# Block products given out between the last layer norm's power and its use, and side sums one product earlier

## The chip, the cores and the metric

The kernel runs on one core of one Trainium2 chip, in one launch. The metric is the device time of an execution in microseconds (us), the median of several runs. An execution taken by the profiler also gives a span, from its first to its last instruction, and a trace of every engine: PE is TensorE's matmuls, PEld its weight loads, DVE VectorE, ACT ScalarE, POOL GpSimd, SP the engine that issues the DMAs.

## What is computed

A transformer block with adaptive layer norm, in float32, on 2048 tokens of width 512:

```python
mod = (_silu(c) @ w_mod).reshape(c.shape[0], 6, 1, -1)      # sa, ca, ga, sb, cb, gb
h = _layernorm(x) * (1 + ca) + sa
x = x + ga * _A_ref(h, A_wqkv, A_wo)                        # linear attention, 32 heads of 16
h = _layernorm(x) * (1 + cb) + sb
x = x + gb * _B_ref(h, B_w_gate, B_w_up, B_w_down)          # ((h W) * (h V)) W2, inner width 1376
```

The second layer norm and the gated feed-forward part behind it are what this case is about.

## The kernel before

**Split products.** A float32 operand is split into a high part, rounded to float32r, the type in which TensorE multiplies it, and a low part, the rest (`split`, L182): ACT makes the high part, DVE or GpSimd the low one. A product of two split operands is three matmuls: high by high, low by high, high by low.

**Tiles.** The 2048 tokens are four chunks of 512 (`ch` 0 to 3), each of four tiles of 128 tokens. The inner width of 1376 is eleven column groups of up to 128.

**The feed-forward blocks.** For most column groups gate and up projections are not computed as eight quarter products, but as seven, in the manner of Strassen and Winograd, over a pair of chunks (0, 1) or (2, 3): sums and differences of quarters of the left operand (`Left`, L743: s1 to s4, the "side sums") and of the weights (`Right`, L792). `block` (L856) is one column group for one pair of chunks. It gives out seven products, P1 to P7, with a `yield` behind each; a product is one call of `times` (L833), six matmuls of 128x512 at L838. They accumulate in four banks a, b, c, d of PSUM, which P1 to P7 write in the order a, d, b, a, c, d, c. Between them stand

- `copy(b, a)` after P1, `copy(p5, d)` after P2, `copy(c, b)` and a copy into `u2` after P3: ACT, L843;
- after P5 `p5 = c + p5` (DVE, L893), after P6 `u2 = d + u2` (DVE, L897);
- after P6 and P7 the multiplications of gate and up, `mul(a, u2)` and `mul(c, p5)` (DVE, L866), whose results are split (`kh` on ACT L183, `kl` on DVE L184) only in the next block, after its first bank copy (`flush`).

So P1 of a block can overwrite bank a only when `mul(a, u2)` of the block before has read it, P5 can accumulate in c only when `copy(c, b)` is done, and P7 can only when `p5 = c + p5` has read c.

At named points behind the products (`p1`, `p5`, `p6`, `p2`, `p7`, `p3`, `p4` in the order P1 to P7) other work is hung in: at `p6` the scaling of the next down weights (DVE, L985), at `p7` the loads for coming blocks and the split of the next block's weights (ACT L817 and L820, GpSimd L824), at `p3` the split of the down weights (ACT L183, GpSimd L184), at `p4` the weight sums (GpSimd, L806). The blocks are called b0, b1, b2, ... here; the kernel counts them in `m`.

**The order is written out by hand.** Each engine works through its own queue in the order in which the program gives the instructions out; semaphores hold an instruction until its operands are there, and all behind it on that engine wait with it. `fill(n)` (L1015) gives out the next n products of the feed-forward blocks, with what hangs at their points, in the middle of other code. It is used while the last chunk's layer norm is under way (L1153 to L1165):

```python
    y_b(15)
    norm2[3].rstd_of()
    norm2[3].nmr_of()
    fill(2)
    norm2[3].xhat(0)
    fill(2)
    norm2[3].xhat(1)
    fill(1)
    norm2[3].xhat(2, 3)
    fill(2)
    ln2_turn(3, 0, 1)
    fill(1)
    ln2_turn(3, 2, 3)
```

`y_b` takes the last attention tile out of PSUM and its statistics. `rstd_of` (L228) adds epsilon on DVE (`ve`, L233) and raises to the power -1/2 on GpSimd (`rstd`, L234). `nmr_of` (L236) makes minus mean times that, on DVE (`nmr`, L237). `xhat` (L240) normalizes a tile of tokens on ACT (L243). `ln2_turn` (L727) transposes two of the four column quarters on TensorE (L250, into two PSUM banks), applies scale and shift on ACT (`f`, L262) and, for this chunk, stores them to DRAM (`kept`, L264, a DMA in SP's queue).

Behind this, the left operands of the second pair of chunks are loaded back from `kept` (eight loads `f`, L110, in SP's queue; a load of a stored piece waits until the store has landed), and their side sums, splits and stores for later are put into a list, `trickle` (L1166). Portions of that list, one entry each, are given out by `some` (L963) at several points of each of the blocks b2 to b6: the first entry is s1 of the first half, a DVE addition (L756) of two loaded pieces, the first and the third of the four that the code above stores. In b2 the points `p1` and `p5` are left out.

From b2 on, blocks are followed by down products (L914 to L916).

Of the kernel before, what the change touches and what calls it, by code (L numbers as in the profile page):

```python
# [22 lines left out]
def tile_adaln_block(  # L23
# [162 lines left out]
    def split_raw(raw, shape=(P, D), low=None):  # L186
        h = B("w", shape, F32R)
        l = B("w", shape, F32R)
        split(raw, h[:raw.shape[0]], l[:raw.shape[0]], low)
        return h, l  # L190
# [425 lines left out]
    def y_b(i):  # L616
        ch, j = divmod(i, NJ)
        ps = yps.pop(i)
        nc.scalar.activation(xts[ch][j], ps, AF.Copy)
        norm2[ch].stats(j, of=ps)  # L620
# [160 lines left out]
    def fetch(stash, side, *names):  # L781
        for n in names:
            side[n] = []
            for k in range(KH):
                side[n].append(tuple(B("h", dt=F32R) for _ in range(2)))
                for part, x in enumerate(side[n][k]):
                    nc.sync.dma_start(f32(x), stash[n, k, part])
# [64 lines left out]
    def flush():  # L852
        while todo:
            todo.pop(0)()

    def block(A, R, out, at):  # L856


        n, R = R.n, R.of
        a, b, c, d = (x[:n] for x in banks)  # L860

        def T2(tag):
            return B(tag)[:n]

        def mul(ps, x):
            nc.vector.tensor_tensor(x, ps, x, op=ALU.mult)  # L866
            todo.append(lambda: out.append(split_h(x, n)))

        def also(point):
            for do in at.get(point, ()):  # L870
                do()

        times(a, A["a11"], R["b11"], True)
        copy(b, a)
        flush()
        also("p1")
        yield
        times(d, A["s1"], R["t1"], True)
        p5 = T2("u")
        copy(p5, d)  # L880
        also("p5")
        yield
        times(b, A["s2"], R["t2"], False)
        copy(c, b)
        u2 = T2("u")
        copy(u2, b)
        also("p6")
        yield
        times(a, A["a12"], R["b21"], False)
        also("p2")  # L890
        yield
        times(c, A["s3"], R["t3"], False)
        nc.vector.tensor_tensor(p5, c, p5, op=ALU.add)  # L893
        also("p7")
        yield
        times(d, A["s4"], R["b22"], False)
        nc.vector.tensor_tensor(u2, d, u2, op=ALU.add)  # L897
        mul(a, u2)
        also("p3")
        yield  # L900
        times(c, A["a22"], R["t4"], False)
        mul(c, p5)
        also("p4")
        yield

    def down_group(ch, side, js, outs, ds, last, by_tile=False, end=False):

        hs = [out[side] for out in outs]

        def mm(ps, i, j, c, d):  # L910
            (hh, hl), (dh, dl) = hs[i], ds[i]
            a, b = j * P, (j + 1) * P
            n = hh.shape[0]
            nc.tensor.matmul(ps, hh[:, a:b], dh[:n, c:d], start=i == 0, stop=False)  # L914
            nc.tensor.matmul(ps, hh[:, a:b], dl[:n, c:d], start=False, stop=False)  # L915
            nc.tensor.matmul(ps, hl[:, a:b], dh[:n, c:d], start=False, stop=i == len(hs) - 1)  # L916

        dn = {j: acc_bank() for j in js}
        tail = js[-1:] if end else []
        order = [(i, j) for i in range(len(hs)) for j in js if j not in tail]  # L920
        if by_tile:
            order.sort(key=lambda ij: ij[1])
        for i, j in order:
            mm(dn[j], i, j, 0, D)

        def take():
            evac(ch, dn, [j for j in js if j not in tail], last)
            for j in tail:
                other = acc_bank()
                for ps, c, d in ((dn[j], 0, D // 2), (other, D // 2, D)):  # L930
                    for i in range(len(hs)):
                        mm(ps[:, c:d], i, j, c, d)
                    evac(ch, {j: ps}, [j], last, ((c, d),))
        return take
# [6 lines left out]
    def right_load(n):  # L941
        if n < len(steps):
            rights[n] = Right(steps[n][1])

    def right_sums(n, on=None):
        if n < len(steps):
            rights[n].sums(on)

    def right_split(n, on=None):
        if n < len(steps):  # L950
            rights[n].high()
            rights[n].lows(on)
# [3 lines left out]
    def draw_load(n):  # L956
        if n < len(steps):
            f0, k = fts[steps[n][1]]
            draws[n] = load(w_down[f0:f0 + k, :], "raw")
# [3 lines left out]
    def some(count):  # L963
        for _ in range(min(count, len(trickle))):
            trickle.pop(0)()
# [6 lines left out]
    def ffn():  # L972

        first_side, second_side = side, {}
        m = 0
        for g, (cs, fs) in enumerate(groups):
            last = g + 1 == len(groups) or groups[g + 1][0] != cs
            outs, ds = [], []
            A = first_side if cs == (0, 1) else second_side
            for f in fs:  # L980
                out = []
                draw = draws.pop(m)

                def scale(d=draw):
                    nc.vector.tensor_tensor(d, d, gb[:d.shape[0]], op=ALU.mult)  # L985

                at = {"p6": [scale],
                      "p7": [lambda: draw_load(m + 1), lambda: right_load(m + 2), lambda: right_split(m + 1)],
                      "p3": [lambda: ds.append(split_raw(draw, low=nc.gpsimd))],
                      "p4": [lambda: right_sums(m + 2)]}  # L990
                for point in ("p1", "p5", "p2", "p3", "p4")[2 if m == 2 else 0:]:
                    at.setdefault(point, []).append(lambda: some(some_at.get(m, 0)))
                if m + 1 < len(steps) and steps[m + 1][0] != cs:
                    at["p1"].append(lambda: fetch(stash, second_side, "a11", "s1"))
                    at["p7"].insert(0, lambda: fetch(stash, second_side, "s2", "a12", "s3"))
                elif m and steps[m - 1][0] != cs:
                    at["p1"].append(lambda: fetch(stash, second_side, "s4", "a22"))
                outs.append(out)
                yield from block(A, rights[m], out, at)
                m += 1  # L1000
                if free[0] and parts:
                    takes = [down_group(*p) for p in parts.pop(0)]
                    yield
                    for take in takes:
                        take()
            cut_at = {2: ([[0, 1, 2, 3], []], [[], [0, 1, 2, 3]]),
                      3: ([[0, 1, 2], []], [[3], [0, 1]], [[], [2, 3]])}[len((groups + groups[-1:])[g + 1][1])]
            parts.extend([(ch, i, js, outs, ds, last) for i, (ch, js) in enumerate(zip(cs, jss)) if js] for jss in cut_at)
        flush()
        while parts:  # L1010
            group = parts.pop(0)
            for p in group:
                down_group(*p, by_tile=not parts, end=not parts and p is group[-1])()

    def fill(n):  # L1015
        for _ in range(n):
            next(work, None)
# [121 lines left out]
    draw_load(0)  # L1139
    stash, some_at = {}, {m: 1 for m in range(2, 7)}  # L1140
    work = ffn()
    y_step(14, seed=None)
    fill(1)
# [8 lines left out]
    fill(2)  # L1152
    y_b(15)  # L1153
    norm2[3].rstd_of()
    norm2[3].nmr_of()
    fill(2)
    norm2[3].xhat(0)
    fill(2)
    norm2[3].xhat(1)
# [38 lines left out]
```

## Time and profile before

| what | value |
|---|---|
| median of 3 runs | 570.62 us (570.37 to 571.47) |
| the profiled execution | 570.02 us |
| its span | 568.3 us |
| mean granted TensorE clock | 0.999 |
| TensorE matmuls | 560.3 us busy, 99% of the span, 2575 instructions |
| VectorE | 373.1 us, 66% |
| ScalarE | 279.8 us, 49% |
| GpSimd | 186.2 us, 33% |

Rows of a timeline give the start and the length in us from the span's start, then engine, line, operation, result and operands by the program's names, shapes, the number of instructions merged into the row, and in brackets the idle time of that engine ahead of it with the instruction that ended it. A matmul's end is modelled and matmuls are pipelined, so consecutive rows of TensorE overlap by a fraction of a microsecond; starts are the safer numbers. Rows of the waits give the line that waited, the line it waited for, and total us, number of times and longest. Rows of DMAs give what is moved, the number, KB each, and the us from issue to landing.

The edited place lies at about 285 to 308 us of the span: b0's last product, b1, and b2.

### The profile page before, as it was taken

What the parts mean: (1) busy time and instruction counts of PE and PEld (TensorE: products, weight loads), DVE (VectorE), ACT (ScalarE), POOL (GpSimd) and SP (SyncE); (2) the same over time, 40 slices, a digit from 0 to 9 for tenths busy, and PEclk for the clock granted to TensorE, in tenths of its full rate; (3) what the DMA queues carried; (4) which work ended last, traced back from release to release, by engine and by line L of the source; (5) the groups of instructions that cost most, each with busy time, mean ns of one, the idle gap of its engine ahead of it and who ended that gap; (6) DMA issues with size and microseconds to landing.
All of it is one profiled execution on the core that took longest, in us unless ns stands there. A gap on an engine that the chain in (4) does not pass through costs nothing.

```text
span 568.3 us, 7356 instructions
## 1 busy us (share of the span) xinstructions
PE 560.3 (99%) x2575; PEld 458.8 (81%) x2575; DVE 373.1 (66%) x614; ACT 279.8 (49%) x500; POOL 186.2 (33%) x191
## 2 busy tenths in 40 slices
PE   8999999999999999999989999999999999999997
PEld 6778888888888878878878888787888888888886
DVE  7876868868768876759767777745554434344445
ACT  3785857546456546445865545534333333334110
POOL 2000000000011300000579666665667446556200
PEclk9999999999999999999999999999999999999999
DMA  8900223302301000804208553599336012200004
GB/s 289 374 3 2 74 75 110 114 0 62 93 0 47 29 1 37 260 0 149 57 2 277 180 190 104 202 348 330 115 111 178 26 57 55 57 19 2 0 1 148
DMA packets 50309, 59.34 MB, mean 104 GB/s; under 512 B 6432, under 2 KB 27168, under 8 KB 50272
## 3 DMA queue, kind: packets, MB, share of 16 engines
q1 hardware_dynamic: 50272, 58.87, 32.1%
q8 instruction: 20, 0.33, 0.2%
q14 instruction: 17, 0.14, 0.1%
HBM read 43.12 MB, written 15.73 MB: 104 GB/s over the span
## 4 chain that ended last, share of the span: by engine, by line
PE 89%; DMA 3%; issue 2%; POOL 1%; DVE 1%; ACT 1%; SPq 1%; POOLq 0%; ACTq 0%
PE bank L838 28%; PE acc L914 6%; PE acc L915 6%; PE acc L916 6%; PE acc L614 6%; PE bank L198 5%; PE bank L196 5%; PE bank L197 5%; PE acc L329 3%; PE acc L327 3%; PE acc L328 3%; PE bank L693 2%; PE bank L691 2%; PE bank L692 2%; PE bank L250 2%
## 5 line engine op out<-in xcount | busy, mean ns | idle before, releaser
L838 PE MATMUL bank<-h,w 128*128 128x512 f32 (+1 forms) x798 | 185.5, 390 | 1.8 <-ACT bank L843 1.2
L838 PEld LDWEIGHTS bank<-h,w 128*128 128x128 f32 (+1 forms) x798 | 148.2, 186 | 35.3 <-ACT bank L843 1.7
L843 ACT ACTIVATE bank<-bank 128x512 f32<-128x512 f32 (+1 forms) x38 | 22.1, 583 | 144.8 <-PE bank L838 144.8
L678 DVE TENSOR_TENSOR x<-acc,x 128x512 f32<-128x512 f32 (+1 forms) x73 | 49.1, 684 | 49.0 <-PE acc L916 48.2
L824 POOL TENSOR_TENSOR w<-raw,w 128x256 fp32r<-128x256 f32 (+3 forms) x38 | 42.4, 1117 | 106.4 <-ACT w L817 86.4
L184 POOL TENSOR_TENSOR w<-raw,w 128x512 fp32r<-128x512 f32 (+1 forms) x25 | 34.9, 1399 | 116.0 <-DVE mv L226 87.6
L914 PE MATMUL acc<-w,kh 128*128 128x512 f32 (+2 forms) x154 | 59.6, 387 | 0.0
L915 PE MATMUL acc<-w,kh 128*128 128x512 f32 (+2 forms) x154 | 59.6, 387 | 0.0
L916 PE MATMUL acc<-w,kl 128*128 128x512 f32 (+2 forms) x154 | 59.5, 386 | 0.0
L234 POOL TENSOR_TENSOR rstd<-ve,half 128x4 f32<-128x4 f32 (+1 forms) x9 | 9.4, 1044 | 126.0 <-DVE ve L233 124.5
L184 DVE TENSOR_TENSOR kl<-u,kh 128x512 fp32r<-128x512 f32 (+1 forms) x38 | 26.8, 746 | 33.1 <-ACT kh L183 31.2
L824 POOL TENSOR_TENSOR w<-t,w 128x512 fp32r<-128x512 f32 (+1 forms) x38 | 48.4, 1293 | 0.0
L196 PE MATMUL bank<-w,h 128*128 128x512 f32 x112 | 45.0, 402 | 0.0
L198 PE MATMUL bank<-w,h 128*128 128x512 f32 x112 | 43.9, 392 | 0.0
L197 PE MATMUL bank<-w,h 128*128 128x512 f32 x112 | 43.6, 389 | 0.0
L614 PE MATMUL acc<-w,xh 128*128 128x512 f32 x120 | 38.1, 399 | 0.0
L914 PEld LDWEIGHTS acc<-w,kh 128*128 128x128 f32 (+1 forms) x154 | 28.9, 188 | 6.0
L916 PEld LDWEIGHTS acc<-w,kl 128*128 128x128 f32 (+1 forms) x154 | 28.9, 188 | 5.9
L915 PEld LDWEIGHTS acc<-w,kh 128*128 128x128 f32 (+1 forms) x154 | 28.9, 188 | 5.9
L893 DVE TENSOR_TENSOR u<-bank,u 128x512 f32<-128x512 f32 (+1 forms) x19 | 13.1, 690 | 30.0 <-PE bank L838 30.0
L243 ACT ACTIVATE n<-x,nmr,rstd 128x512 f32<-128x512 f32 x32 | 24.1, 804 | 17.2 <-DVE nmr L237 15.9
L262 ACT ACTIVATE f<-bank,col,col 128x512 f32<-128x512 f32 x28 | 20.7, 775 | 14.5 <-PE bank L250 12.4
(177 smaller groups left out, 1105.1 us busy)
## 6 DMA issues: line engine op xcount, KB each, us to landing
raw<-in_w_mod_dram SPq DMA_DIRECT2D x24, 256.0 KB, 3.7
raw<-in_B_w_down_dram SPq DMA_DIRECT2D x20, 256.0 KB, 2.9
raw<-in_B_w_gate_dram SPq DMA_DIRECT2D x36, 128.0 KB, 3.7
raw<-in_B_w_up_dram SPq DMA_DIRECT2D x36, 128.0 KB, 3.6
x<-in_A_x_dram SPq DMA_DIRECT2D x16, 256.0 KB, 5.4
kept<-f SPq DMA_DIRECT2D x16, 256.0 KB, 2.0
f<-kept SPq DMA_DIRECT2D x16, 256.0 KB, 4.8
side_s<-h SPq DMA_DIRECT2D x16, 256.0 KB, 2.6
```

Source lines behind the costliest of these rows:

```text
L184: (low or nc.vector).tensor_tensor(l, src, f32(h), op=ALU.subtract)
L196: nc.tensor.matmul(ps, ah, bh, start=i == 0, stop=False)
L197: nc.tensor.matmul(ps, ah, bl, start=False, stop=False)
L198: nc.tensor.matmul(ps, al, bh, start=False, stop=i == n - 1)
L243: nc.scalar.activation(self.n[j], self.tiles[j], AF.Identity, scale=self.rstd[:, j:j + 1], bias=self.nmr[:, j:j + 1])
L614: nc.tensor.matmul(yps[i], x, y, start=False, stop=k == KD - 1 and x is al, skip_group_check=True)
L678: nc.vector.tensor_tensor(xt[:, a:b], dn[j][:, a:b], xt[:, a:b], op=ALU.add)
L824: sub = lambda out, x, y: (on or nc.gpsimd).tensor_tensor(out, x, f32(y), op=ALU.subtract)
L838: mm = lambda x, y, **kw: nc.tensor.matmul(ps, x[:, k], y, skip_group_check=True, **kw)
L914: nc.tensor.matmul(ps, hh[:, a:b], dh[:n, c:d], start=i == 0, stop=False)
L915: nc.tensor.matmul(ps, hh[:, a:b], dl[:n, c:d], start=False, stop=False)
L916: nc.tensor.matmul(ps, hl[:, a:b], dh[:n, c:d], start=False, stop=i == len(hs) - 1)
```

## The change

```diff
@@ -988,7 +988,7 @@
                       "p4": [lambda: right_sums(m + 2)]}
-                for point in ("p1", "p5", "p2", "p3", "p4")[2 if m == 2 else 0:]:
+                for point in ("p1", "p5", "p6", "p3", "p4")[2 if m == 2 else 0:]:
                     at.setdefault(point, []).append(lambda: some(some_at.get(m, 0)))
@@ -1152,8 +1152,9 @@
     fill(2)
     y_b(15)
     norm2[3].rstd_of()
+    fill(3)
     norm2[3].nmr_of()
-    fill(2)
+    fill(1)
     norm2[3].xhat(0)
     fill(2)
     norm2[3].xhat(1)
```

Two things are moved.

The portions of `trickle` that stood behind P4 (`p2`) stand behind P3 (`p6`), there behind the scaling of the down weights.

Three products are given out between `rstd_of` and `nmr_of`, and one, no longer two, between `nmr_of` and the first `xhat`. In all, sixteen products are given out by `fill` up to the end of this code, where it was fourteen, so that everything from `nmr_of` on comes later in the order of products:

| given out | before | after |
|---|---|---|
| between `rstd_of` and `nmr_of` | none | P7 of b0, P1 and P2 of b1 |
| between `nmr_of` and `xhat(0)` | P7 of b0, P1 of b1 | P3 of b1 |
| between `xhat(0)` and `xhat(1)` | P2, P3 of b1 | P4, P5 of b1 |
| between `xhat(1)` and `xhat(2, 3)` | P4 of b1 | P6 of b1 |
| between `xhat(2, 3)` and the first two transposes | P5, P6 of b1 | P7 of b1, P1 of b2 |
| between these and the last two transposes | P7 of b1 | P2 of b2 |

No instruction is added or taken away on any engine.

## Prediction

> **What bounds the kernel now.** I read the page's engine line first, then TensorE's waits, then the timelines of single engines around the edit. A "product" below is one `times` call (six matmuls, L838); P1 to P7 are the seven of a block, b0, b1, b2 the first three blocks.
>
> ```profile
> PE 560.3 (99%) x2575; PEld 458.8 (81%) x2575; DVE 373.1 (66%) x614; ACT 279.8 (49%) x500; POOL 186.2 (33%) x191
> ```
>
> ```profile
> PE bank L838 <- ACT bank L843: 1.2, 1, 1.2
> PE bank L257 <- ACT n L243: 0.5, 1, 0.5
> PE bank L838 <- DVE u L866: 0.3, 1, 0.3
> ```
>
> TensorE (PE) is busy 99% of the span, and of its few waits (total us, times, longest) the two for bank copies and multiplications at L838 lie at the edit. So the time is the matmuls plus the few places where TensorE stands still: what an edit saves or adds there goes into the time one to one, and what it does to other engines counts only through TensorE.
>
> ```profile
> 280.68 4.24 PE L838 MATMUL bank<-h,w 128*128 128x512 f32 x18
> 285.23 5.72 PE L838 MATMUL bank<-h,w 128*128 128x512 f32 x24 [0.31 <-DVE u L866]
> 292.19 3.02 PE L838 MATMUL bank<-h,w 128*128 128x512 f32 x12 [1.24 <-ACT bank L843]
> 295.04 1.03 PE L250 MATMUL acc<-ident,n 128*128 128x128 f32 x8
> 295.83 1.63 PE L838 MATMUL bank<-h,w 128*128 128x512 f32 x6
> 297.30 1.03 PE L250 MATMUL acc<-ident,n 128*128 128x128 f32 x8
> 298.09 9.83 PE L838 MATMUL bank<-h,w 128*128 128x512 f32 x42
> 307.76 0.39 PE L914 MATMUL acc<-w,kh 128*128 128x512 f32 x1
> ```
>
> TensorE's timeline (start, length, form, count; idle before it and who ended that). Rows overlap by the pipeline's tail, so I work with starts. The 42 matmuls of b2 take 307.76 - 298.09 = 9.67 us, 0.230 each, 1.38 a product. At this pace the 24 from 285.23 (P1 to P4 of b1) make room for P5 at 290.75; it starts at 292.19. That is 1.44 us of standstill. Likewise b0's last 18 matmuls end at 284.82 and b1's P1 starts at 285.23: 0.41 us.
>
> Who makes P5 late? DVE, then ACT, in order of time:
>
> ```profile
> 284.39 0.69 DVE L866 TENSOR_TENSOR u<-bank,u 128x512 f32<-128x512 f32 x1
> ...
> 285.94 0.34 DVE L233 TENSOR_SCALAR ve<-mv 128x4 f32<-128x4 f32 x1
> 288.50 0.69 DVE L237 SCALAR_TENSOR_TENSOR nmr<-mv,rstd 128x4 f32<-128x4 f32 x1 [2.23 <-POOL rstd L234]
> 289.12 0.68 DVE L866 TENSOR_TENSOR u<-bank,u 128x512 f32<-128x512 f32 x1
> ```
>
> ```profile
> 286.95 0.58 ACT L843 ACTIVATE bank<-bank 128x512 f32<-128x512 f32 x1 [3.43 <-PE bank L838]
> 287.44 0.62 ACT L183 ACTIVATE kh<-u 128x512 fp32r<-128x512 f32 x1
> 289.83 0.63 ACT L183 ACTIVATE kh<-u 128x512 fp32r<-128x512 f32 x1 [1.76 <-DVE u L866]
> 290.37 0.80 ACT L243 ACTIVATE n<-x,nmr,rstd 128x512 f32<-128x512 f32 x1
> 291.07 0.57 ACT L843 ACTIVATE u<-bank 128x512 f32<-128x512 f32 x1
> 291.55 0.58 ACT L843 ACTIVATE bank<-bank 128x512 f32<-128x512 f32 x1
> ```
>
> `nmr_of` (L237) stood 2.23 us in DVE's queue for GpSimd's power. Behind it stood the last product of b0 (L866 at 289.12), behind that ACT's second `kh` (289.83), behind that the first `xhat` and the bank copy that P5 needs (291.55 to 292.13, P5 at 292.19).
>
> **The change part by part.** The program's order, engine by engine, has the same instructions before and after; only places differ. The other edit (side sums at P3, not P4) moves nothing: between the two points stand only TensorE's six matmuls of P4, so DVE, ACT and the DMA queue get their instructions in the same order as before. Its cost is 0, whatever hides it.
>
> *What goes.* `nmr` now stands behind L866 and both `kl` of b0. The power ends at about 288.5 (where `nmr` starts), and by then DVE has work. ACT's queue becomes 286.95 copy, two `kh` to 288.5, then the copy for P5, 0.34 after the product ahead of it ends (b1's P1 ends 286.61, its copy starts 286.95): 290.75 - 1.38 + 0.34 = 289.71, ended 290.29. P5 can start at 290.75: **-1.44 us**. The cover for the power is L866 and the two `kl`, to about 289.4 (the first `kh` ends at 288.06, two `kl` of some 0.7 behind it); it is gone if the power ends later than that, or if ACT's `xhat` gets ahead of the copy, which its order excludes.
>
> *What comes between blocks.* Before, the second four columns of transposes (297.30) lay between b1's P7 and b2's P1 and covered DVE's multiplication L866. Now P1 follows P7 directly, as between b0 and b1, where that cost 0.41. So P5 to P7 run from 290.75 to 294.89, P1 of b2 starts at 295.30: **+0.41 us**. Both transpose groups cost 0.88 each as before (297.30 to 298.09, and 0.09 ahead), one after P1 (296.68 to 297.56), one after P2 (298.94 to 299.82). The first needs all four `xhat`s:
>
> ```profile
> 292.54 2.21 ACT L243 ACTIVATE n<-x,nmr,rstd 128x512 f32<-128x512 f32 x3
> 294.66 0.41 ACT L817 ACTIVATE w<-raw 128x256 fp32r<-128x256 f32 x1
> ...
> 296.53 0.62 ACT L183 ACTIVATE w<-raw 128x512 fp32r<-128x512 f32 x1
> 297.05 2.77 ACT L262 ACTIVATE f<-acc,col,col 128x512 f32<-128x512 f32 x4
> 299.82 0.58 ACT L843 ACTIVATE bank<-bank 128x512 f32<-128x512 f32 x1
> 300.32 1.14 ACT L183 ACTIVATE kh<-u 128x512 fp32r<-128x512 f32 x2
> 301.36 0.59 ACT L843 ACTIVATE u<-bank 128x512 f32<-128x512 f32 x1
> ```
>
> An `xhat` takes 0.71 (three from 292.54 to 294.66), the weight copies of L817 and L820 that now stand behind the first one 1.87 (to 296.53), the `w` split 0.52. From 290.7, when the three bank copies are done, the last `xhat` ends at 290.7 + 4 x 0.71 + 1.87 + 0.52, near 296.0: 0.7 us ahead of its use, and P3 of b2 starts at 299.82. Before it was 298.09 + 2.76 = 300.85. So far TensorE leads by 1.03 us.
>
> *What is late next.* Behind the transposes hang ACT's L262, the stores of the four `f` to DRAM, the loads of the side sums' inputs from there, and the first side sum (L756) on DVE.
>
> ```profile
> 299.17 0.32 SPq L264 DMA_DIRECT2D kept<-f  x1
> ```
>
> ```profile
> 301.29 0.32 SPq L110 DMA_DIRECT2D f<-kept  x1
> ```
>
> ```profile
> f<-kept SPq DMA_DIRECT2D x1, 256.0 KB, 3.4
> ```
>
> ```profile
> 304.80 0.77 DVE L756 TENSOR_TENSOR s<-f,f 128x512 f32<-128x512 f32 x1 [0.38 <-DMA f<-kept]
> 305.49 0.68 DVE L893 TENSOR_TENSOR u<-bank,u 128x512 f32<-128x512 f32 x1
> ...
> 307.99 1.23 DVE L756 TENSOR_TENSOR s<-f,f 128x512 f32<-128x512 f32 x1
> 309.14 0.68 DVE L866 TENSOR_TENSOR u<-bank,u 128x512 f32<-128x512 f32 x1
> ```
>
> The third `f` is the one that counts: evicted from 298.43 (third of four, 0.69 each), stored at 299.17, its load issued 2.12 us later at 301.29 (the load waits for the store to land), landed 3.4 us later at 304.69, and L756, which DVE was already waiting for (0.38 us idle), starts at 304.80. Right behind it in DVE's queue stands L893, which reads bank c for `p5`; P7 of b2 overwrites bank c, so it waits for L893. L893 ended at 306.17; with 0.15 us to TensorE (284.39 + 0.69 to 285.23) that is 306.32, and P7's turn came at 298.09 + 6 x 1.38 = 306.37. **The chain had 0.05 us to spare.**
>
> Afterwards ACT copies b2's P1 at 296.68 + 0.34 = 297.02, does two `kh` (to 298.56, by the steps 299.82, 300.32, 301.36), two L262 (to 299.94), and then, because P2 is given out between the transposes, the copy for `p5` (0.5 us), and only then the third L262: 300.44, which is 2.01 us later than 298.43. Everything behind it moves with it: the store from 299.17 to 301.18, the sum from 304.80 to 306.81, L893 to 307.50 to 308.18, P7 to 308.33. TensorE could give it out at 299.82 + 4 x 1.38 = 305.34 and stands still for 3.0 us. Against 306.37 before, P7 is **1.96 us later**. The sum is the same: -1.44 + 0.41 + 2.99 = +1.96.
>
> Nothing behind takes it back: the down projection and b3 have their operands earlier than TensorE needs them, and TensorE is the bound to the end.
>
> The bounds. If b2's P1 doesn't lose the 0.41 us, ACT's chain starts as much earlier: +1.55. The sum's length depends on GpSimd: 0.69 us from its start to the next DVE instruction in the one row, 1.15 in the other (307.99 to 309.14, GpSimd busy). With the longer one it is +2.42. Both together give +1.55 to +2.42; I take 1.96, from the row of this very instruction. If two more such delays hit the chain it is +2.9.
>
> The Trainium skill (SBUF — State Buffer, "Who interferes with whom") says that a VectorE instruction with two SBUF inputs and a GpSimd instruction that reads SBUF exclude each other for the whole of the earlier one. The 1.23 us of the row at 307.99 agree with it; by the rule the sum would be held for one GpSimd instruction at most, and the time would be near my upper bound.
>
> **The sum against the runs.** The profiled execution took 570.02 us (span 568.3), and with 1.96 comes to 572.0. The timed runs have a median of 570.62, 0.60 above the profiled one, the lowest 0.35 above; I add 0.5 and predict 572.5.
>
> **The rivals.**
>
> *The gain alone.* The store and load of the third `f` come back sooner than in this trace, so that L893 isn't held. For it: two of the four stores now go ahead by more, so the third queues behind less. Against: behind the third nothing changes, and of the 5.5 us from store to landing 3.0 would have to vanish. Then -1.03: 569.6 on the scale of the timed runs. The chain decides at 3.0 us; below that each us counts.
>
> *Half of it.* The wait is there but shorter by 1 to 1.5 us (the load's 3.4 us contain the queue of seven others): +0.5 to +1.0, 571.3.
>
> *A cold array.* TensorE stands still for 3.0 us, twice as long as ahead of P5 now; should its clock drop after that, as it does not here during 1.4:
>
> ```profile
> 290.60:292.20 1.60, 0.36 (x3) 0.02 (x1) 1.60 (x2) 1.60 (x4) 1.60 (x2) 1.00 0.02 5
> ```
>
> (busy time by engine, then the granted clock, 1.00), and halve for as long as the gap lasted, 3.0 us of work would lose 1.5: 574.0. The Trainium skill (TensorE: Matmul & The Clock Gate, "What's actually happening") has such a rule, with an idle window of about 3.4 us; a gap of 3.0 would just stay under it, and nothing in this trace shows what a longer one does.
>
> *The change doesn't do what it says.* `nmr` might still hold something: but by the time the power is ready it still has 0.9 us of other DVE work ahead of it, so the 1.44 us are the safest term. Were they not won, all would come 1.44 later: 573.9.
>
> **How the numbers follow.** The forecast, 571.6 to 573.4 by its own bounds and the runs' scatter: 0.77. Half of it: 0.10. The gain alone: 0.07. A cold array: 0.04. The change not doing what it says: 0.02. The range 571.0 to 573.6 leaves out the gain, the cold array and part of the half. About 0.2%, 1.1 us, is what a measurement of this kernel can tell from no change, so 571.76 is the border: slower 0.76 (most of the forecast and the cold array), within 0.2% 0.16 (the half and the forecast's lower end), faster 0.08.
>
> **What would show it.** Right: no wait of `nmr` for the power and P5 of b1 at 290.7; 0.4 us ahead of b2's P1; DVE idle for the load of `f` for over 2 us ahead of L756 near 306.8; TensorE idle near 3 us ahead of b2's P7, released by L893. Wrong: L893 of b2 near 304.5 with no DMA wait ahead, or a clock under 1.00 after the gap, or a new wait at P5 of b2 (the copy of L843, which I have ending at 302.4, 0.2 us ahead of its use).

## The result, and the profile after

| | before | after |
|---|---|---|
| median | 570.50 us (6 runs, 569.61 to 571.47) | 574.02 us (6 runs, 571.61 to 574.80) |
| ratio, 95% interval | | 1.0056 [1.0036, 1.0076] |
| the profiled execution, its span | 570.02 us, 568.3 us | 573.47 us, 571.8 us |
| mean granted clock, by run | 0.999 in the profiled one | 1.000 (571.61 us), 0.997 (573.47, 574.02, 574.03, 574.33), 0.994 (574.80) |

The change costs 3.5 us. The forecast was 572.5 with a range up to 573.6: the direction was right, and the time lies outside the range.

The engine line of the changed kernel and TensorE's waits (line that waited, line waited for, total us, times, longest):

```profile
PE 561.0 (98%) x2575; PEld 459.2 (80%) x2575; DVE 371.7 (65%) x614; ACT 279.6 (49%) x500; POOL 185.1 (32%) x191
```

```profile
PE bank L838 <- DVE u L893: 3.3, 1, 3.3
...
PE bank L838 <- DVE u L866: 0.6, 2, 0.3
```

The 1.2 us for the bank copy (L843) are gone, and a single wait of 3.3 us for L893 has come. TensorE's timeline of the changed kernel shows both places, and a third thing (start, length, form, count, idle before):

```profile
280.50 4.24 PE L838 MATMUL bank<-h,w 128*128 128x512 f32 x18
285.05 9.81 PE L838 MATMUL bank<-h,w 128*128 128x512 f32 x42 [0.31 <-DVE u L866]
295.17 1.61 PE L838 MATMUL bank<-h,w 128*128 128x512 f32 x6 [0.31 <-DVE u L866]
...
299.67 5.73 PE L838 MATMUL bank<-h,w 128*128 128x512 f32 x24
308.70 2.13 PE L838 MATMUL bank<-h,w 128*128 128x512 f32 x6 [3.30 <-DVE u L893]
310.63 0.63 PE L914 MATMUL acc<-w,kh 128*128 128x512 f32 x1
311.06 0.63 PE L915 MATMUL acc<-w,kh 128*128 128x512 f32 x1
...
313.15 0.39 PE L914 MATMUL acc<-w,kh 128*128 128x512 f32 x1
```

All 42 matmuls of b1 run from 285.05 without a stop: the gain is there. The 24 of b2's P3 to P6 make room for P7 at 299.67 + 4 x 1.375 = 305.17, and it starts at 308.70: a gap of 3.53 us. The third thing is the rows behind it: the down matmuls start 0.43 us apart (310.63, 311.06) and have a length of 0.63, where at 313.15 it is 0.39. TensorE works at half speed for a while, as the windows of the changed kernel say (stretch, its length, PE busy and matmuls, granted clock, share and GB/s of the DMAs):

```profile
305.00:308.70 3.70, 0.40 (x2) 1.00 0.97 342
308.70:309.30 0.60, 0.60 (x3) 1.00 1.00 355
309.30:313.10 3.80, 3.80 (x11) 0.55 0.86 275
313.10:317.30 4.20, 4.20 (x20) 1.00 0.00 1
```

From P7 to the first product of b3 it is 317.25 - 308.70 = 8.55 us, against 313.20 - 306.37 = 6.83 before: the lower clock costs 1.72 us.

Who holds P7 up stands in DVE's timeline of the changed kernel, with GpSimd's and the DMA queue's rows beside it:

```profile
287.93 1.84 DVE L184 TENSOR_TENSOR kl<-u,kh 128x512 fp32r<-128x512 f32 x2 [1.25 <-ACT kh L183]
289.69 0.70 DVE L237 SCALAR_TENSOR_TENSOR nmr<-mv,rstd 128x4 f32<-128x4 f32 x1
...
306.70 1.34 DVE L756 TENSOR_TENSOR s<-f,f 128x512 f32<-128x512 f32 x1 [5.19 <-DMA f<-kept]
307.97 0.68 DVE L893 TENSOR_TENSOR u<-bank,u 128x512 f32<-128x512 f32 x1
```

```profile
306.24 1.26 POOL L824 TENSOR_TENSOR w<-raw,w 128x512 fp32r<-128x512 f32 x1
```

```profile
301.04 0.32 SPq L264 DMA_DIRECT2D kept<-f  x1
```

```profile
303.11 0.32 SPq L110 DMA_DIRECT2D f<-kept  x1
```

`nmr` has no wait any more. The first side sum waits 5.19 us for its input from DRAM, with L893 behind it; it is itself nearly twice as long as before (1.34 for 0.77) with GpSimd's L824 at work over the same time.

The span's 3.5 us are then: P7 of b2 later by 308.70 - 306.37 = 2.33, the low clock 1.72, and 0.59 that come back in b6. There before had a stop of 0.28 us ahead of P7, and after has none:

```profile
358.14 8.35 PE L838 MATMUL bank<-h,w 128*128 128x512 f32 x36
366.77 1.65 PE L838 MATMUL bank<-h,w 128*128 128x512 f32 x6 [0.28 <-DVE u L893]
373.72 9.68 PE L838 MATMUL bank<-h,w 128*128 128x512 f32 x42
```

```profile
362.19 9.71 PE L838 MATMUL bank<-h,w 128*128 128x512 f32 x42
377.18 8.10 PE L838 MATMUL bank<-h,w 128*128 128x512 f32 x35
```

(before first, then after: from b6's first product to the next block's it is 15.58 us in the one and 14.99 in the other). 2.33 + 1.72 - 0.59 = 3.46.

### The profile page after: what moved, and what is told of

It is laid out like the page before. It is cut to its first block, busy times and chain, and to the rows that moved or that the text cites. A ratio compares the mean times of both kernels' runs of the same rounds, so it can differ in the third digit from the quotient of the medians.

```text
span 571.8 us, 7362 instructions
## 1 busy us (share of the span) xinstructions
PE 561.0 (98%) x2575; PEld 459.2 (80%) x2575; DVE 371.7 (65%) x614; ACT 279.6 (49%) x500; POOL 185.1 (32%) x191
## 4 chain that ended last, share of the span: by engine, by line
PE 93%; DMA 4%; DVE 1%; ACT 1%; SPq 1%; issue 0%; DVEq 0%; ACTq 0%
PE bank L838 30%; PE acc L614 7%; PE acc L914 6%; PE acc L915 6%; PE acc L916 6%; PE bank L198 5%; PE bank L196 5%; PE bank L197 5%; PE acc L329 3%; PE acc L327 3%; PE acc L328 3%; PE bank L693 2%; PE bank L691 2%; PE bank L692 2%; PE bank L250 2%; DMA raw<-in_A_wqkv_dram 2%
## 5 line engine op out<-in xcount | busy, mean ns | idle before, releaser
L843 ACT ACTIVATE bank<-bank 128x512 f32<-128x512 f32 (+1 forms) x38 | 22.2, 584 | 151.0 <-PE bank L838 151.0
L824 POOL TENSOR_TENSOR w<-raw,w 128x256 fp32r<-128x256 f32 (+3 forms) x38 | 42.0, 1107 | 107.3 <-ACT w L817 87.4
L184 POOL TENSOR_TENSOR w<-raw,w 128x512 fp32r<-128x512 f32 (+1 forms) x25 | 34.9, 1398 | 116.0 <-DVE mv L226 87.5
L184 DVE TENSOR_TENSOR kl<-u,kh 128x512 fp32r<-128x512 f32 (+1 forms) x38 | 27.1, 755 | 34.0 <-ACT kh L183 32.1
L824 POOL TENSOR_TENSOR w<-t,w 128x512 fp32r<-128x512 f32 (+1 forms) x38 | 47.9, 1279 | 0.0
L893 DVE TENSOR_TENSOR u<-bank,u 128x512 f32<-128x512 f32 (+1 forms) x19 | 13.1, 691 | 29.7 <-PE bank L838 29.7
L183 ACT ACTIVATE w<-raw 128x512 fp32r<-128x512 f32 (+2 forms) x44 | 26.4, 618 | 2.6 <-DMA raw<-in_A_wqkv_dram 1.6
```

Source lines behind the costliest of these rows:

```text
L183: nc.scalar.activation(h, src, AF.Copy)
L184: (low or nc.vector).tensor_tensor(l, src, f32(h), op=ALU.subtract)
L824: sub = lambda out, x, y: (on or nc.gpsimd).tensor_tensor(out, x, f32(y), op=ALU.subtract)
```

## Experiments

The theory tested: everything that the products' move puts later lets the side sum's input come too late, the sum holds L893 and with it P7, and the gap is long enough for TensorE's clock to drop; stall and clock cost about the same. The rivals: the loss is in the other edit (portions at P3); the clock's drop is chance and the stall costs everything; or a different wait further back costs it. The ratios are to the kernel before, with 95% intervals.

### One edit at a time

`e1_point_alone` is the kernel before with the portions at P3 and nothing else:

```diff
-                for point in ("p1", "p5", "p2", "p3", "p4")[2 if m == 2 else 0:]:
+                for point in ("p1", "p5", "p6", "p3", "p4")[2 if m == 2 else 0:]:
```

> Only the first hunk: the side sums' portions behind P3 instead of P4, on the kernel before. Theory A (the wait of the third block's P7 for the side sum, then the halved clock, both from the later transposes): no instruction changes its place on an engine, so 570.5 us, within 0.3 of before, and no TensorE wait above 1.3 us. Rival B (the earlier point makes the sum stand ahead of L893 and is the cause): +3 us, 573.5, with DVE waiting over 2 us for the load of f.

Measured: 570.52 us, 0.9997 [0.9988, 1.0005]. The portions' move does nothing that these runs can tell.

`e2_fill_alone` is the kernel before with the products moved and the portions left at P4:

```diff
     norm2[3].rstd_of()
+    fill(3)
     norm2[3].nmr_of()
-    fill(2)
+    fill(1)
     norm2[3].xhat(0)
```

> Only the second hunk: three products between the power and its use, portions as before. Theory A: all of the loss, 573.5 to 574.5 us, TensorE waiting 3.3 us for L893 and a mean clock of 0.994 to 0.997 in most runs. Rival B: the gain alone, 569.5, clock 1.000.

Measured: 573.87 us, 1.0055 [1.0038, 1.0072]; TensorE waits for L893 once, as in after:

```profile
PE bank L838 <- DVE u L893: 3.3, 1, 3.3
```

So the whole loss is the products' move, and the portions' point neither hurts nor helps. The time scatters by its clock: 572.11 and 572.16 at 1.000, 573.42 at 0.997, 574.32 to 574.98 at 0.994.

`e11_after_again` is the changed kernel once more, without an edit.

> The changed kernel once more, beside the two others on the same chip, for the share of runs with a lowered clock: two thirds or more at 0.994 to 0.997 and above 573, the rest at 1.000 and near 572.1 (as the runs so far: seven of nine timed above 573).

Measured: 573.57 us, 1.0052 [1.0033, 1.0072]: one run at 1.000 (570.69), four at 0.997 (573.39 to 573.63), two at 0.994 (574.88 and 575.52). (The count in the expectation is a slip: in the result's runs and those of `e2_fill_alone` it was nine of twelve above 573.) A drop of the clock is no chance event of one profile; it belongs to this kernel.

### The stall with and without the clock

Three kernels put spare matmuls ahead of b2's P7, into a PSUM bank that is free there; their result is used by nothing. They shorten TensorE's standstill without touching the chain that releases P7:

```diff
+    def spare(A, R, count):
+        ps = acc_bank()
+        (bh, bl), (ah, al) = R["b22"], A["s4"][0]
+        for _ in range(count):
+            nc.tensor.matmul(ps[:bh.shape[-1]], bh[:, 0], ah, start=True, stop=True)
...
+                if m == 2:
+                    at["p3"].append(lambda: spare(A, rights[2].of, 8))
```

`e4_spare8` is the changed kernel with eight of them.

> The changed kernel with eight spare matmuls into an unused bank ahead of b2's P7 (1.84 us of TensorE work inside the 3.5 us gap; their result is used by nothing). Theory A: P7 starts at the same 308.7, the gap left is 1.7 us, the clock stays 1.000 and the 24 matmuls behind take 0.23 us each: 572.3 us, 1.7 less than the changed kernel, though TensorE does more. Rival C: the clock falls all the same, 574. Rival D (no clock effect, the stall is all of it): 574, clock as in the changed kernel.

Measured: 572.12 us (571.97 to 573.02), 1.0032 [1.0020, 1.0044], the clock 0.999 or 1.000 in all five runs. Its TensorE timeline, then its window behind the stop:

```profile
305.30 1.98 PE L974 MATMUL acc<-h,w 128*128 128x512 f32 x8
308.84 1.65 PE L838 MATMUL bank<-h,w 128*128 128x512 f32 x6 [1.57 <-DVE u L893]
310.33 0.39 PE L914 MATMUL acc<-w,kh 128*128 128x512 f32 x1
```

```profile
308.84:313.10 4.26, 4.26 (x19) 1.00 0.87 283
```

P7 starts no earlier than in after (308.84), and TensorE has done eight matmuls more, yet the kernel is 1.5 to 1.9 us faster than after and its repetitions (572.12 against medians of 573.57 to 574.02): 19 matmuls in 4.26 us where after did 11 in 3.80. This tells stall and clock apart. The stall alone costs about 1.5 us by the runs (572.12 against 570.64 for before in the same series), the clock the rest.

`e6_spare2` and `e10_spare5` have two and five spare matmuls.

> The changed kernel with two spare matmuls ahead of b2's P7 instead of eight: the gap is 3.53 - 0.46 = 3.07 us. If a gap must cover a window of 3.4 us, the clock stays 1.000 in all runs and the time is that of e4_spare8, 572.1. If the clock needs less idle time, it falls in some runs, to 0.997, and those take 573.5 to 574.5.

> The changed kernel with five spare matmuls ahead of b2's P7: a gap of 2.4 us, between e4_spare8 (1.7 us, clock 1.000 in five of five runs) and e6_spare2 (3.1 us, three of six runs at 0.997). If the chance of a halved clock grows with the gap, one or two runs in six fall to 0.997 and 573.5, the median is 572.2; if there is an edge between 2.4 and 3.1, none.

Measured: with two 573.16 us, 1.0045 [1.0032, 1.0057], three runs at 1.000 (572.13, 572.30, 572.95) and three at 0.997 (573.38, 573.48, 573.64); with five 571.99 us, 1.0030 [1.0017, 1.0043], seven runs at 1.000 and two at 0.997 (573.60, 574.03). The profiled runs are both at the full clock, with these stops (two, then five; the spare matmuls, then P7):

```profile
305.66 0.61 PE L974 MATMUL acc<-h,w 128*128 128x512 f32 x2
309.19 1.65 PE L838 MATMUL bank<-h,w 128*128 128x512 f32 x6 [2.91 <-DVE u L893]
```

```profile
305.80 1.29 PE L974 MATMUL acc<-h,w 128*128 128x512 f32 x5
309.32 1.66 PE L838 MATMUL bank<-h,w 128*128 128x512 f32 x6 [2.23 <-DVE u L893]
```

These counts show no sharp edge at one length of the gap: the drop becomes likelier as the gap grows. The table stands in the last section.

### Taking the sum out of P7's way

`e3_late_sum` is the changed kernel with the first portion of b2 at `p3`, behind P6, where L893, L897 and the first multiplication already stand ahead of it:

```diff
-                for point in ("p1", "p5", "p6", "p3", "p4")[2 if m == 2 else 0:]:
+                for point in ("p1", "p5", "p6", "p3", "p4")[3 if m == 2 else 0:]:
```

> The changed kernel, but in b2 the portions start at p3, behind L893, L897 and the first multiplication, so that the same wait for the load of f holds nothing that P7 needs. Theory A: DVE still waits for the load to about 306.7, but P7 of b2 starts at 305.2 without a stop, the clock stays 1.000, and what is left is 1.44 us won less 0.41 lost: 569.5 us. Rival C (the clock falls by itself, or the loss sits in the order of the transposes): 571.5 to 574, clock under 1.

Measured: 570.80 us (568.92 to 573.74), 1.0006 [0.9991, 1.0021]. The stop ahead of P7 is gone; from this kernel's TensorE timeline:

```profile
301.03 7.06 PE L838 MATMUL bank<-h,w 128*128 128x512 f32 x30
```

Thus the side sum is the cause of the stall, as its order in DVE's queue is all that changed ahead of P7. But the whole list of portions is one place later from here on, and a stored left operand arrives late at the second pair of chunks, a new row in the waits:

```profile
PE bank L838 <- DMA h<-side_a: 0.6, 1, 0.6
```

In the profile the block with that wait takes 1.29 us longer than in before (388.87 to 403.94 against 388.68 to 402.46), and b3's P7 stops for 0.34 us. The expected 569.5 was missed by 1.3. Two of its twelve runs had a clock of 0.997 (572.83 and 573.74); where in them, their times alone do not tell.

`e5_late_sum_two` keeps that and gives out two portions at `p4` of b2, behind P7, so that the list isn't late afterwards:

```diff
+                if m == 2:
+                    at["p4"].append(lambda: some(1))
```

> As e3_late_sum (the first side sum of b2 behind L893), but p4 of b2 gives two portions, so that the list is where the changed kernel has it from b3 on. Theory A with what e3 left: e3's median was held back by portions that came one place later everywhere and reached the loads of the second pair of chunks late (0.6 us of TensorE waiting for h<-side_a); here that is gone, no run has a clock under 0.999, and the median is 569.4 us, 1.1 under before. Rival C (the new order of transposes costs as such): 570.5 or more.

Measured: 570.12 us, 0.9997 [0.9987, 1.0007], the clock 0.999 or 1.000 in all twelve runs. In its profile b3 starts 0.96 us ahead of before when both are counted from b0's first row here (312.59 - 281.03 against 313.20 - 280.68), as expected from the prediction's 1.03. But then b3's P7 stops:

```profile
312.59 8.32 PE L838 MATMUL bank<-h,w 128*128 128x512 f32 x36
321.14 1.66 PE L838 MATMUL bank<-h,w 128*128 128x512 f32 x6 [0.23 <-DVE u L893]
```

with a split of a side sum ahead of L893 on DVE, 1.23 us long. The queue's pattern repeats itself one block later, at a smaller price: b3 takes 0.54 us longer than in before (312.59 to 328.09 against 313.20 to 328.16). So the loss of 3.5 us is wiped out, but the lead isn't kept: 0.7 short of what was expected.

`e7_early_pair` leaves the sum where it is and lets its input come earlier: of the four column quarters the first and third are transposed and stored first, and their loads issued at once.

```diff
-    ln2_turn(3, 0, 1)
+    ln2_turn(3, 0, 2)
+    lefts = [Left((2, 3), 0)]
     fill(1)
-    ln2_turn(3, 2, 3)
-    for k in range(KH):
-        trickle += Left((2, 3), k).aside(stash).steps()
+    ln2_turn(3, 1, 3)
+    lefts.append(Left((2, 3), 1))
+    for left in lefts:
+        trickle += left.aside(stash).steps()
```

> The changed kernel with column quarters 0 and 2 transposed first, and the first half's four loads issued ahead of the last two quarters' stores. Theory A (the way from the second needed f through DRAM to the side sum sets P7): that f is evicted about 1.9 us earlier, the sum starts near 305 us, the gap shrinks from 3.5 to about 1.7 us, no clock loss: 570.3 to 570.8 us. Rival D (the round trip isn't what holds the sum): as the changed kernel, 574.

Measured: 572.47 us (570.77 to 574.61), 1.0037 [1.0022, 1.0051]. Its TensorE timeline:

```profile
306.48 1.65 PE L838 MATMUL bank<-h,w 128*128 128x512 f32 x6 [0.90 <-DVE u L893]
...
324.30 2.93 PE L838 MATMUL bank<-h,w 128*128 128x512 f32 x6 [2.55 <-DVE u L893]
```

At b2 it does what was expected: with the input 1.7 us earlier (the sum starts at 305.04, not 306.70) the stop falls from 3.30 to 0.90. But the other half's loads wait in SP's queue and go out four at a time later:

```profile
308.65 1.91 SPq L110 DMA_DIRECT2D f<-kept  x4
```

The weights' loads come behind them, and GpSimd waits for those:

```profile
316.08 0.74 POOL L806 TENSOR_TENSOR t<-raw 128x256 f32<-128x256 f32 x1 [6.18 <-DMA raw<-in_B_w_up_dram]
```

It works beside DVE's splits, and L893 of b3 keeps P7 waiting for 2.55 us. The granted clock falls just before P7 starts:

```profile
324.00:326.00 2.00, 1.70 (x4) 0.51 0.69 207
326.00:328.00 2.00, 2.00 (x7) 0.63 0.83 229
```

The fastest four runs (570.77 to 570.99) are near what was expected, the median isn't. In the profiled execution the stall was moved by one block.

### Keeping the gain without the loss

If the theory is right, the gain of 1.44 (`nmr` behind the power) doesn't need the transposes to move. `e8_nmr_alone` is the kernel before with three products between the power and `nmr`, and as many fewer behind it, so that the transposes stay at their products:

```diff
     norm2[3].rstd_of()
+    fill(3)
     norm2[3].nmr_of()
-    fill(2)
+    fill(1)
     norm2[3].xhat(0)
-    fill(2)
-    norm2[3].xhat(1)
     fill(1)
-    norm2[3].xhat(2, 3)
+    norm2[3].xhat(1, 2, 3)
     fill(2)
```

> The kernel before with three products between the power and its use, but the transposes, stores and loads at their old products (one product between the first and second xhat, the other three xhats together). Theory A: the 1.44 us ahead of P5 of b1 are won, nothing is given back, since the store, the load and b2's P7 all move forward together: 569.1 us, clock 1.000, no TensorE wait above 0.5 us in the blocks. Rival C (any product ahead of nmr costs later): 570.5 or more.

Measured: 568.99 us, 0.9970 [0.9959, 0.9982]. The cost of 3.5 us becomes a gain of 1.3 (568.99 against 570.29 for before in the same series). What is left of the stall stands in its TensorE and DVE timelines; the sum waits 0.62 us for its input, where after waits 5.19. The expectation of no wait above 0.5 us in the blocks was missed, as P7 of b2 still stands for 0.70:

```profile
296.86 8.45 PE L838 MATMUL bank<-h,w 128*128 128x512 f32 x36
306.01 1.66 PE L838 MATMUL bank<-h,w 128*128 128x512 f32 x6 [0.70 <-DVE u L893]
```

```profile
304.13 1.22 DVE L756 TENSOR_TENSOR s<-f,f 128x512 f32<-128x512 f32 x1 [0.62 <-DMA f<-kept]
```

`e9_nmr_late` takes that away as well, with the portions of `e5_late_sum_two` (points as before, `p2`):

```diff
-                for point in ("p1", "p5", "p2", "p3", "p4")[2 if m == 2 else 0:]:
+                for point in ("p1", "p5", "p2", "p3", "p4")[3 if m == 2 else 0:]:
                     at.setdefault(point, []).append(lambda: some(some_at.get(m, 0)))
+                if m == 2:
+                    at["p4"].append(lambda: some(1))
```

> e8_nmr_alone with b2's first side sum given out behind L893, L897 and the first multiplication (and two portions at p4, as in e5_late_sum_two). In e8 P7 of b2 still stood 0.7 us idle behind that sum, which GpSimd had stretched to 1.22 us. Theory A: this stop goes too, 568.1 us; if b3 gets the stop of 0.4 us that e5 had there, 568.5. If the sum's place isn't what holds P7, 569.0 as e8.

Measured: 567.98 us (567.50 to 568.38), 0.9958 [0.9946, 0.9971], faster than both kernels. Its interval and that of `e8_nmr_alone` overlap, so the runs don't tell these two apart; the stop itself is gone. Of the stops in the blocks, TensorE's timeline has only the 0.31 us at b1 left:

```profile
284.75 8.43 PE L838 MATMUL bank<-h,w 128*128 128x512 f32 x36 [0.31 <-DVE u L866]
...
296.06 9.81 PE L838 MATMUL bank<-h,w 128*128 128x512 f32 x42
```

## Why the prediction was right in its direction and wrong in its time

**The bound and what goes** held. TensorE sets the time; P5 of b1 no longer stops, and the 1.44 us are there: b1's 42 matmuls are one row.

**What comes between blocks** held: b2's P1 has the same 0.31 us of idle time as b1's.

**The portions' edit costs nothing** held: `e1_point_alone`, 0.9997.

**What is late next** held in place and order. Behind the third `f` the store was predicted at 301.18 and came at 301.04, the sum at 306.81 and came at 306.70. `e3_late_sum` and `e7_early_pair` show that it is this sum and this input: a later sum removes the stop, an earlier input shrinks it to 0.90 us.

**The sum's length was mis-sized.** From the sum's start to L893 I took 0.69 us from the row of before; it was 307.97 - 306.70 = 1.27, above the upper bound of 1.15 as well. The sum moved into the time of GpSimd's L824 (306.24 to 307.50). In before it started at 304.80 and met only the last 0.2 us of a GpSimd instruction (first row); another sum of after runs while GpSimd does nothing (second row):

```profile
303.83 1.18 POOL L806 TENSOR_TENSOR t<-raw,t 128x256 f32<-128x256 f32 x1
```

```profile
309.89 0.68 DVE L756 TENSOR_TENSOR s<-f,f 128x512 f32<-128x512 f32 x1
```

The Trainium skill (SBUF — State Buffer, "Who interferes with whom") has the rule for it, and the rows agree: 0.68 us without such company, 1.09 to 1.77 beside GpSimd in the rows of after, `e8_nmr_alone` and `e9_nmr_late`. With 1.27 in place of 0.69 the prediction's own sum gives +2.54, and after shows 2.51 when both kernels are counted from b0's row (308.70 - 280.50 against 306.37 - 280.68). The better choice was to look what GpSimd does at the new time of the sum, not at the old.

**"A gap of 3.0 would just stay under it"** is the step that failed. The rival of the cold array got 0.04 and stayed outside the sum and the range, and it is what happened in 15 of the 19 runs of after and of its products' move alone. It failed in two ways: the gap was 3.53 us for the reason above, and the clock drops for shorter gaps too (`e6_spare2`: in three of six runs at 3.07; in the profile of `e7_early_pair` after 2.4). "A clock under 1.00 after the gap" stood among the prediction's signs of being wrong, and it came. The rival's price of 1.5 us was near the 1.72 measured, but by luck: it let the clock stay low for as long as the gap had lasted, and in the four profiles with a drop it stays low for 3.4 us, in `e7_early_pair` too, where the gap was 2.6. With 1.72, +2.54 + 1.72 less the next point's 0.59 is +3.67 on the prediction's scale, beside 3.5 measured.

**"Nothing behind takes it back"** was wrong by 0.59 us: b6 before had a stop of its own at P7 (0.28 us of idle time in its row), which the prediction didn't look at since it stands 60 us behind the edit. There the split ahead of L893 on DVE (L184) took 1.22 us in before, where GpSimd's L824 had started 0.07 us ahead of it, and 0.69 us in after, where L824 started 0.29 us behind it: the same pattern as the sum's. What shifted the two against each other wasn't tried. This 0.59 and the 0.58 by which the sum was mis-sized cancel by chance, so what is left of the miss, 574.0 against 572.5, is the clock's drop.

One thing stays open. The runs of after, of `e2_fill_alone` and of `e11_after_again` at a clock of 1.000 (570.69, 571.61, 572.11 and 572.16) lie 0.1 to 1.5 us above the before of their series, where `e4_spare8`, with the stall alone, lies 1.5 above. Single runs of one kernel scatter by about as much: `e10_spare5`, whose P7 is as late, has 571.00 to 572.92 at a clock of 1.000. Only 570.69 lies below that. Whether its gap was shorter is not known; none of the four was profiled.

## What to carry to other kernels

Before an instruction is moved, look in each engine's queue for one that waits for a DMA and stands ahead of the one that frees a buffer: the time it has to spare (0.05 us here) is the real budget of the move, and what is saved upstream can be had without touching it, as `e8_nmr_alone` and `e9_nmr_late` do. Where the operands of a waiting instruction come late, price it beside its new neighbours, not its old ones. And where a predicted stall of TensorE nears 2 to 3 us, put the clock's drop into the sum, not into a footnote: here it doubled the price.

## What the runs showed of the hardware

How often TensorE's clock drops after a gap in its work, by the runs' mean granted clock (0.997 or 0.994 against 0.999 or 1.000). The gap is from the last matmul's slot to the next start in each kernel's profile:

| kernel | gap in the profile, us | runs with a lowered clock |
|---|---|---|
| `e4_spare8` | 1.7 | 0 of 5 |
| `e10_spare5` | 2.4 | 2 of 9 |
| `e6_spare2` | 3.1 | 3 of 6 |
| after, `e2_fill_alone`, `e11_after_again` | 3.5 | 15 of 19 |

The gaps of the runs that weren't profiled may differ from these, and where in a run the clock fell is known only from a profile. The 2 of 9 alone prove little: `e3_late_sum` had 2 of 12 without a stop at this place, and before had 1 of 62 in the three series. But in the profile of `e7_early_pair` the clock falls inside a stop: the first of its windows above holds 2.00 x (1 - 0.51) / 0.5 = 1.96 us at half clock, so the drop comes at 324.04, 2.4 us behind the last matmul's slot (313.42 + 36 x 0.229 = 321.67) and 0.26 ahead of P7.

The time at half clock was the same there (1.96 and, from the second window, 1.48 us: 3.4) and in all three profiles of the 3.5 us gap. In after it is 3.80 x (1 - 0.55) / 0.5 = 3.4 us, which costs half of that, the 1.72 us seen; in `e11_after_again`, with a mean of 0.53 over 3.60 us, it is 3.4 as well. A finer window of after shows where the drop comes:

```profile
309.00:310.00 1.00, 1.00 (x5) 0.83 1.03 391
```

That is (1 - 0.83) / 0.5 = 0.34 us at half clock, so it comes at 309.66, 0.96 us behind the start of P7. In `e2_fill_alone` the clock fell already before the work came back; its windows:

```profile
308.00:308.90 0.90, 0.00 (x0) 0.75 0.88 296
308.90:309.50 0.60, 0.57 (x1) 0.50 1.05 348
309.50:311.60 2.10, 2.10 (x6) 0.50 1.05 372
311.60:313.00 1.40, 1.40 (x7) 0.91 0.81 222
```

That is 0.45 + 0.60 + 2.10 + 0.25 = 3.4 us again, of which 0.45 fell into the gap and cost nothing. The point of the drop isn't tied to the gap's start or end, then: 0.96 us behind the end of the gap in after, about 0.45 ahead of it here. The Trainium skill (TensorE: Matmul & The Clock Gate, "What's actually happening") has windows of about 3.4 us that run on by themselves, and that agrees with both the length and the moving start. Read as a window without any matmul, its idle window does not agree, and the runs decide: the 3.4 us up to after's drop hold 0.96 us of matmuls, and in `e7_early_pair` the clock fell after 2.4 us without one. How much idle time is enough, the runs don't settle. A run at 0.994 has lost as much as two such windows (0.006 x 572 = 3.4 us, against 1.7 at 0.997); how that comes about was not seen in a profile.
